# The causal mask of a recurrence's softmax moves from TensorE to VectorE

## The chip, the cores and the metric

One core of one Trainium2 chip runs the kernel. The time is that of the whole kernel on the device, in microseconds (us), as the median of several runs. The engines are called PE (TensorE; PEld is its weight load), DVE (VectorE), ACT (ScalarE), POOL (GpSimd) and SP (SyncE, which here only issues DMAs).

## What is computed

Two attentions over the same x (2048 tokens, 576 features), mixed by a gate. Part A is a recurrence over 64 segments of 32 tokens: each segment attends, together with 8 memory rows, over 40 positions, and the first 8 rows of its output are the next segment's memory. Part B is plain attention with 32 heads of width 18 over all 2048 tokens.

```python
L = M + seg_len                                   # 8 + 32
mask = (idx[:, None] < M) | (idx[:, None] >= idx[None, :])
for s in range(n_seg):                            # 64, one after the other
    h = concat([mem, xs])                         # 40 x 576
    q, k, v = h @ Wq, h @ Wk, h @ Wv              # 32 heads of 128
    scores = where(mask, q @ k.T * scale, -1e9)
    o = (softmax(scores) @ v) @ Wo
    mem = o[:M]
g = sigmoid((x * gate_w).sum(-1, keepdims=True))
return g * A(x) + (1 - g) * B(x)
```

## The kernel before

Everything is recorded first as operations of a planner (`Plan.add`: a name, the engine or engines that may do it, a duration, what it depends on) and then issued. The order on each engine is not found at run time: `ORDER` holds, for PE, DVE, ACT, POOL and SP, a list of numbers that is the sequence of operations (where an operation may go to two engines, the list that it stands in decides). `Plan.run` walks these lists with its constants and durations (`LATE`, `LAG`, `RATES` and those given to `add`), and from this it decides two things only: which operations on PE take the full form of the array and which four columns of 32, and where PE gets a **filler**. `Plan.zeros` adds a filler, one group of matmuls with zero weights on the open sum of part B (L1036 in four columns, L1042 in the full form), wherever by its reckoning PE would stand for at least the filler's length and a margin.

The first 150 us load x and the weights, project part B's q, k and v and write them to memory in DRAM. Then the recurrence runs, some 17.7 us for each of its 64 segments, to about 1285 us, and part B's visits are laid into it: 512 visits of four heads, each of them four score matmuls (L1065, into `sb` and `sp`), two exponentials on ACT (L1074, L1078), four matmuls on the values (L1088, into `ob`). Also in PE's list are the pieces of `last_unit` (L1156, L1160), projections of the last 8 tokens of each segment, which need no memory and are done ahead. At the end the outputs are mixed and stored.

A segment of the recurrence, with the names that the rows show:

- `pvv` (L1437): Q, K and V in pieces, four column groups of 128x32; the tails of the features go in a form of their own (64 rows).
- Q and K are transposed on DVE from `pvv` to `tf` (L1478) and cast into `qk` on POOL or DVE (L1524); V goes through `tm` (L660 on DVE, L658 on ACT) to `v_sb` (L1501, POOL or DVE).
- `psh`: scores, in two halves of 16 heads. One PE step holds the mask's product (L1538, four matmuls of `ident` with `veil`, 320 columns each) and 32 small products (L1546) added to it.
- `et` (L1556): the exponential on ACT, 128x320 in bf16. `pss` (L1567 or L1572): its column sums on PE; `rq` (L1584): reciprocal on DVE; `prb` (L1592): PE spreads it; `et` times `prb` on DVE (L1603).
- `pso` (L1614): weights times V on PE; `ot`: a cast on DVE or ACT; `acc` (L1319): times Wo; `sum` and `obf` (L1346, L1647) add the parts on DVE; `pw` (L1662, L1669): PE turns the new memory, DVE puts it in `ht` (L1678), and the next segment starts.

`veil` is made once: zeros, and -30000 where the mask is false, so that the exponential of a masked score is 0:

```python
nc.tensor.matmul(
    ph[32 * i:32 * i + 32, :], lhsT=ident[:, o:o + 32],
    rhs=veil[:, :].unsqueeze(1).to_broadcast([P, 8, L]),
    start=True, stop=False, ...)
```

DMAs of the loop (`by_head` at L985 for kch, qch and otd; vch, qkd, vld, xg, a_dram) may stand in SP's list or in POOL's.

Of the kernel before, what the change touches and what calls it, by code (L numbers as in the profile page):

```python
# [9 lines left out]
BF16 = mybir.dt.bfloat16  # L10
# [483 lines left out]
def kernel(  # L494
# [15 lines left out]
    nc = tc.nc  # L510
# [1313 lines left out]
    for n in range(NT):  # L1824
        qc, i = divmod(n, 4)
        halves = []
        for hf in range(2):
# [18 lines left out]
            def combine(e, n=n, hf=hf):  # L1846
# [4 lines left out]
                )  # L1851

            halves.append(add(
                f"cb{n}.{hf}", "DVE", psum_copy(288), combine, [a, gates[n]], give=(("pb", a, 0),)
            ))

        def store_out(e, n=n):
# [43 lines left out]
```

## Time and profile before

| what | value |
|---|---|
| runs | 1320.95 us median of 3 (1316.97 to 1321.24) |
| the profiled execution | span 1319.9 us, from its first to its last instruction; no other time of it is given, and the median is 1.05 us above it |
| PE busy | 1287.9 us, 98% |
| ACT busy | 1118.8 us, 85% |
| DVE busy | 796.1 us, 60% |
| POOL busy | 623.2 us, 47% |
[...]

Busy time is the union of an engine's instructions, with the ends of matmuls modelled. What a matmul group takes of PE's queue is therefore read from starts: the distance from its start to that of the next. The idle time of an engine is put down to the instruction that ended it. An engine that idles and is waited for by nobody costs nothing.

### The profile page before, as it was taken

The page shows a single profiled execution, that of the slowest core. Times are in us where ns is not written, and L with a number is a line of the kernel's source. Part 1 is how long each engine was busy: PE and PEld are TensorE (multiplying, and loading weights), DVE is VectorE, ACT ScalarE, POOL GpSimd, SP SyncE. Part 2 cuts the span into 40 slices and gives each one's busy share as a digit, 9 for nine tenths or more (in the row PEclk, how much of TensorE's full clock was granted, in tenths as well). Part 3 has the DMA queues.
Part 4 walks back from the last instruction along what each step waited for, and adds up shares of the span by engine and source line. Part 5 has one row for each costly group of instructions (what it writes and reads, how often), then busy time and mean ns, then how long its engine had stood idle before and what let it go on. Part 6 is the DMA issues. An engine that isn't in the chain of part 4 may idle for free.

```text
span 1319.9 us, 72882 instructions
## 1 busy us (share of the span) xinstructions
PE 1287.9 (98%) x32807; PEld 694.6 (53%) x32807; DVE 796.1 (60%) x1778; ACT 1118.8 (85%) x1343; POOL 623.2 (47%) x1291
## 2 busy tenths in 40 slices
PE   8999999999999999999999999999999999999998
PEld 5444544555555555555555545555555445554445
DVE  3133566666566666655566666666666666666676
ACT  4678989988889888888888888888878989998895
POOL 5461454634653356545553556544436445434430
PEclk9989999999999999999999999999999999999999
DMA  7987512111211022011220112211122111111125
GB/s 233 295 260 245 180 41 57 28 36 33 56 37 42 17 54 57 21 29 35 51 51 26 35 37 45 52 28 34 27 50 64 23 26 25 32 40 23 23 53 182
DMA packets 145064, 88.60 MB, mean 67 GB/s; under 512 B 102439, under 2 KB 135383, under 8 KB 144751
## 3 DMA queue, kind: packets, MB, share of 16 engines
q1 hardware_dynamic: 127527, 51.33, 15.2%
q0 software_dynamic: 15088, 30.41, 7.7%
q8 instruction: 257, 4.21, 1.4%
q10 hardware_dynamic: 2136, 2.19, 0.6%
q14 instruction: 56, 0.46, 0.1%
HBM read 52.74 MB, written 31.12 MB: 64 GB/s over the span
## 4 chain that ended last, share of the span: by engine, by line
PE 86%; DVE 5%; ACT 3%; DMA 3%; issue 2%; POOL 1%; SPq 0%; DVEq 0%; ACTq 0%; POOLq 0%
PE pvv L1437 30%; PE acc L1319 12%; PE sb L1065 11%; PE ob L1088 8%; PE pv L1156 5%; PE pso L1614 3%; PE pq L870 3%; PE pv L1160 3%; ACT etb L1074 2%; PE psh L1546 2%; PE po L1833 1%; PE prb L1592 1%; PE psh L1538 1%; DMA vch<-vgd 1%; DVE v_sb L1501 1%
## 5 line engine op out<-in xcount | busy, mean ns | idle before, releaser
L1074 ACT ACTIVATE etb<-sb 128x1536 bf16<-128x1536 f32 x512 | 743.9, 1453 | 119.6 <-PE sp L1065 89.6
L1078 ACT ACTIVATE etb<-sp 128x512 bf16<-128x512 f32 x512 | 306.4, 598 | 0.8 <-PE sp L1065 0.7
L1501 POOL COPY v_sb<-tm 32x512 bf16<-32x512 bf16 x360 | 224.4, 623 | 140.3 <-DVE tm L660 90.5
L1437 PEld LDWEIGHTS <-ht 128*32 128x32 bf16 (+1 forms) x7680 | 171.6, 94 | 214.4 <-issue 115.0
L1478 DVE STREAM_TRANSPOSE tf<-pvv 128x512 f32<-128x512 f32 x256 | 180.9, 713 | 167.1 <-PE pvv L1437 160.7
L1524 POOL CAST qk<-tf 128x512 bf16<-128x512 f32 x142 | 88.2, 622 | 303.3 <-DVE tf L1478 301.0
L1065 PE MATMUL sb<-qch,kch 32*128 32x512 bf16 x1536 | 201.9, 385 | 4.7 <-ACT etb L1074 2.3
L1065 PE MATMUL sp<-qch,kch 32*128 32x512 bf16 x512 | 196.6, 384 | 2.1 <-DVE vt L660 1.8
L1088 PE MATMUL ob<-etb,vch 128*32 128x512 bf16 x2048 | 193.8, 383 | 1.0 <-DMA vch<-vgd 0.8
L1437 PE MATMUL pvv<-wq_m,ht 128*32 128x512 bf16 x2048 | 163.0, 381 | 0.7
L1437 PE MATMUL pvv<-wk_m,ht 128*32 128x512 bf16 x2048 | 163.0, 381 | 0.2
L1319 PE MATMUL acc<-wo,ot 128*32 128x288 bf16 (+1 forms) x6144 | 160.6, 248 | 1.5 <-DVE ot L660 0.9
L1437 PE MATMUL pvv<-wv_m,ht 128*32 128x512 bf16 x2048 | 155.3, 381 | 0.2
L1319 PEld LDWEIGHTS <-ot 128*32 128x32 bf16 x6144 | 113.8, 97 | 31.9 <-issue 11.7
L1065 PEld LDWEIGHTS <-kch 32*128 32x128 bf16 x2048 | 56.1, 91 | 121.3 <-issue 108.1
L660 DVE CAST ot<-pso 128x320 bf16<-128x320 f32 x192 | 87.6, 485 | 45.9 <-PE pso L1614 44.6
L660 DVE CAST tm<-pvv 128x512 bf16<-128x512 f32 x101 | 69.0, 685 | 46.3 <-PE pvv L1437 43.6
L1088 PEld LDWEIGHTS <-vch 128*32 128x32 bf16 x2048 | 51.6, 95 | 46.2 <-issue 28.5
L1405 POOL COPY qk<-xl 128x128 bf16<-128x128 bf16 x256 | 65.8, 295 | 19.3 <-PE sp L1065 7.5
L1603 DVE TENSOR_TENSOR et<-et,prb 128x320 bf16<-128x320 bf16 x128 | 61.8, 485 | 20.6 <-PE prb L1592 17.4
L1501 DVE COPY v_sb<-tm 32x512 bf16<-32x512 bf16 x152 | 65.6, 432 | 11.7 <-ACT tm L658 9.0
L1556 ACT ACTIVATE et<-psh 128x320 bf16<-128x320 f32 x128 | 55.7, 440 | 17.8 <-PE psh L1546 16.3
(160 smaller groups left out, 1820.6 us busy)
## 6 DMA issues: line engine op xcount, KB each, us to landing
xl<-qkd SPq DMA_DIRECT2D x32, 256.0 KB
qkd<-vl SPq DMA_DIRECT2D x41, 128.0 KB
wo<-in_A_Wo_dram POOLq DMA_DIRECT2D x8, 576.0 KB, 5.8
wq_m<-in_A_Wq_dram POOLq DMA_DIRECT2D x8, 512.0 KB, 6.3
vgd<-vt SPq DMA_DIRECT2D x32, 128.0 KB
wk_m<-in_A_Wk_dram POOLq DMA_DIRECT2D x8, 512.0 KB, 6.9
wv_m<-in_A_Wv_dram POOLq DMA_DIRECT2D x8, 512.0 KB, 6.0
v_sb<-vld SPq DMA_DIRECT2D x128, 32.0 KB
```

What stands on the lines that cost most here:

```text
L660: nc.vector.tensor_copy(out=out_of(), in_=in_of())
L1065: nc.tensor.matmul(sb[:, j, :] if j < 3 else sp[:, :], lhsT=kc[r, o:o + P], rhs=qt_[r, :], start=True, stop=True, tile_position=(32 * j, 0),)
L1074: nc.scalar.activation(out=etb[:, 0:3, :], in_=box["sb", gq, kb][:, :, :], func=ACT.Exp, scale=scale_b)
L1078: nc.scalar.activation(out=etb[:, 3, :], in_=box["sp", gq, kb][:, :], func=ACT.Exp, scale=scale_b)
L1088: nc.tensor.matmul(ob[32 * j:32 * j + 32, :], lhsT=vc[:, o + 32 * j:o + 32 * j + 32], rhs=etb[:, j, :], start=(kb == 0), stop=(kb == NKB - ...
L1156: nc.tensor.matmul(out_, lhsT=lw, rhs=rw, start=(c == 0), stop=(c == NF), skip_group_check=wide)
L1319: nc.tensor.matmul(acc[32 * q:32 * q + 32, :], lhsT=o[:, slot, t0:t0 + CT], rhs=wo[:, h, d:d + n], start=(first and s_ == (s_ % 2 if wide ...
L1405: nc.gpsimd.tensor_copy(out=opened["qk"][:, f, a, 0:16 * L].rearrange("p (u h t) -> p u h t", h=4, t=L)[:, :, :, CT:L], in_=xl[:, f, a, :, ...
L1437: nc.tensor.matmul(o, lhsT=ht[:, c, :], rhs=rw, start=start, stop=stop, tile_position=(r, 32 * j), skip_group_check=True,)
L1478: nc.vector.transpose(out=tf[:, :], in_=box["pvv", s, n][:, :])
L1501: move(out=opened["v_sb"][64 * (j // 2):64 * (j // 2) + CT, o:o + 512], in_=tm[32 * j:32 * j + CT, :],)
L1524: move(out=opened["qk"][:, hf, a, 0:16 * L].rearrange("p (k t) -> p k t", t=L)[:, :, 0:CT], in_=box["tf", s, "QK"[a] + str(hf)][:, :].rear ...
```

## The change

The mask's product leaves the score step: `psh` is 32 matmuls, each of which starts and stops its sum. A constant `cap` takes the place of `veil`: 3.0e38 where the mask is true and 0 where it is false. After the exponential, a new step `kp` on DVE takes the minimum of `et` and `cap`, and the column sums wait for it instead of the exponential. The numbers of `ORDER` and `FULL` are all new, as are some of the planner's constants and durations.

```diff
 ORDER = {
     "PE":
-        "19 15 -5 -5 164 -128 152 -99 -39 210 -159 -75 34 116 -92 -10 45 -3 6 12 -6 -107 10 82 -68 86 -39 33 -21 -49 "
...
     "SP":
...
+        "17 10 14 -2 -2 52 -46 22 22 4 -28 38 -48 24 -10 48 27 12 -27 245 -227 45 -51 234 -225 18 -3 -12 135 -117 3 "
...
-    LAG = {"SP": 0.66, "ACT": 0.66, "POOL": 1.25}
+    LAGS = ({"SP": 0.8, "ACT": 0.8, "POOL": 2.5}, {"SP": 0.66, "ACT": 0.66, "POOL": 1.25})
...
-    RATES = ((300.0, 0.8), (220.0, 0.55))
+    RATES = ((320.0, 1.4), (220.0, 0.55))
...
-    nc.vector.memset(veil[:], 0.0)
+    nc.vector.memset(cap[:], 3.0e38)
...
-        out=veil[0:64, M:L], in_=veil[0:64, M:L], pattern=[[1, seg]],
-        compare_op=ALU.is_gt, fill=-30000.0, base=M + 1, channel_multiplier=-1,
+        out=cap[0:64, M:L], in_=cap[0:64, M:L], pattern=[[1, seg]],
+        compare_op=ALU.is_gt, fill=0.0, base=M + 1, channel_multiplier=-1,
...
+    nc.vector.tensor_copy(out=cap[64:P, :], in_=cap[0:64, :])
...
-                add(f"qd{hf}.{s}", ("DVE", "POOL"), (0.8, 1.33), put_v(hf, (1, 3)), before),
+                add(f"qd{hf}.{s}", ("DVE", "POOL"), (0.9, 1.33), put_v(hf, (1, 3)), before),
...
-                for i in range(4):
-                    o = 32 * (i % 2)
-                    nc.tensor.matmul(
-                        ph[32 * i:32 * i + 32, :], lhsT=ident[:, o:o + 32],
-                        rhs=veil[:, :].unsqueeze(1).to_broadcast([P, 8, L]),
-                        start=True, stop=False, tile_position=(0, 32 * i), skip_group_check=True,
-                    )
...
-                            start=False, stop=True, tile_position=(0, 32 * i), skip_group_check=True,
+                            start=True, stop=True, tile_position=(0, 32 * i), skip_group_check=True,
...
-            p_ = add(f"ph{hf}.{s}", "PE", 0.36, psh, [*turned, pl], mode="col", take=("pb",), pairs=36, drain=0.268)
+            p_ = add(f"ph{hf}.{s}", "PE", 0.227, psh, [*turned, pl], mode="col", take=("pb",), pairs=32, drain=0.268)
...
+            def mask(e, hf=hf):
+                et = opened["et", hf][:, :].rearrange("p (r t) -> p r t", t=L)
+                nc.vector.tensor_tensor(
+                    out=et, in0=et, in1=cap[:, :].unsqueeze(1).to_broadcast([P, 8, L]), op=ALU.min,
+                )
+
+            m_ = add(f"kp{hf}.{s}", "DVE", 0.25, mask, [x_])
...
-            s_ = add(f"sm{hf}.{s}", "PE", 0.08, sm, [x_],
+            s_ = add(f"sm{hf}.{s}", "PE", 0.08, sm, [m_],
...
-            add(f"of{qc}", "SP", 1.9, load_of, [zo, *last["Q"], *deps], dmas=2, kb=590)
+            add(f"of{qc}", "SP", 1.07, load_of, [zo, *last["Q"], *deps], dmas=2, kb=590)
...
-            gates[n] = add(f"ga{n}", ("ACT", "DVE"), (act_time(576), 0.65), mul_a, [la, *last["used"]])
+            gates[n] = add(f"ga{n}", ("ACT", "DVE"), (0.77, 0.51), mul_a, [la, *last["used"]])
```

What this does to the instructions, at three places of the loop. Lines of the changed kernel are a few higher (L1546 becomes L1544, L1592 L1598, L1614 L1620, L1036 L1041, L1603 L1609).

First, DVE in the 51st segment, from the transposes of Q and K to the end of the first half's softmax (`et_1829` and `et_1811` are the first half's tile). Before:

```order
L1478 STREAM_TRANSPOSE tf<-pvv 128x512 x2
L1524 CAST qk<-tf 128x16x32
L1584 RECIPROCAL rq<-pss 107x6
L660 CAST tm<-pvv 128x512
L1603 TENSOR_TENSOR et_1829<-et_1829,prb 128x320
L1501 COPY v_sb<-tm 32x512 x2
```

Now:

```order
L1483 STREAM_TRANSPOSE tf<-pvv 128x512 x2
L1560 TENSOR_TENSOR et_1811<-et_1811,cap 128x320
L1529 CAST qk<-tf 128x16x32
L1590 RECIPROCAL rq<-pss 107x6
L1506 COPY v_sb<-tm 32x512 x2
L1609 TENSOR_TENSOR et_1811<-et_1811,prb 128x320
```

The minimum is new; it waits for ACT's exponential, and the cast to qk that was ahead of this half's reciprocal now stands behind the minimum.

Second, PE at the same place, from the first half's scores to its `pso`; of each group of matmuls the first stands here. Before:

```order
L1546 MATMUL psh<-qk 32x40
...
L1065 MATMUL sb<-qch_120,kch_113 128x512
...
L1437 MATMUL pvv<-wv_m,ht_1817 32x512
...
L1572 MATMUL pss<-bsel,et_1829 32x2
...
L1538 MATMUL psh<-veil,ident 32x320
...
L1592 MATMUL prb<-ident,rq 32x107
...
L1088 MATMUL ob<-etb,vch_116 32x512
...
L1036 MATMUL ob<-ident,nil 32x512
...
L1614 MATMUL pso<-et_1829,v_sb 128x40
```

Now:

```order
L1544 MATMUL psh<-qk 32x40
...
L1442 MATMUL pvv<-wk_m,ht_1799 32x512
...
L1093 MATMUL ob<-etb,vch_113 32x512
...
L1070 MATMUL sb<-qch_117,kch_110 128x512
...
L1041 MATMUL ob<-ident,nil 32x512
...
L1578 MATMUL pss<-bsel,et_1811 32x2
...
L1598 MATMUL prb<-ident,rq 32x107
...
L1620 MATMUL pso<-et_1811,v_sb 128x40
```

The mask's product is gone. Between the scores and the column sums there were one score group and one value piece of V; there are three pieces of K, a values group, a score group and two fillers. A third filler stands between `prb` and `pso`, where there was one.

Third, POOL in the 23rd segment, between two copies of x into `ht`. Before:

```order
L1386 COPY ht_1817<-xg 128x5x24
L1501 COPY v_sb<-tm 32x512 x2
L1524 CAST qk<-tf 128x16x32
L1501 COPY v_sb<-tm 32x512 x6
L1386 COPY ht_1819<-xg 128x5x24
```

Now:

```order
L1391 COPY ht_1799<-xg 128x5x24
L1218 DMA vld<-vl 128x512 x2
L1506 COPY v_sb<-tm 32x512 x2
L1019 DMA vch_115<-vgd 128x4x128
L1720 DMA a_dram<-lbf 4x8x144 x4
L1220 DMA qkd<-vl 128x512
L1506 COPY v_sb<-tm 32x512 x2
```

Eight DMA issues stand there that SP's list held before.

## Rows read from the trace of the kernel before

**Rows 1.** The core's span and its mean granted TensorE clock.

```profile
core 0: 1319.9 us, clock 0.996
```

**Rows 2.** The page: busy us, share of the span, instructions of each engine.

```profile
PE 1287.9 (98%) x32807; PEld 694.6 (53%) x32807; DVE 796.1 (60%) x1778; ACT 1118.8 (85%) x1343; POOL 623.2 (47%) x1291
```

**Rows 3.** Windows: stretch, its length, busy us of each engine, clock, DMA share, GB/s.

```profile
0.00:40.00 40.00, 34.28 (x235) 21.26 (x236) 13.65 (x65) 15.39 (x30) 20.44 (x56) 1.00 0.83 249
40.00:125.00 85.00, 80.62 (x709) 37.93 (x709) 24.53 (x64) 67.67 (x81) 31.89 (x68) 0.96 0.83 269
125.00:150.00 25.00, 24.91 (x397) 14.78 (x398) 11.81 (x27) 22.41 (x24) 6.82 (x12) 1.00 0.63 200
150.00:1285.00 1135.00, 1118.53 (x31082) 600.42 (x31074) 721.78 (x1570) 992.40 (x1187) 562.34 (x1153) 1.00 0.17 39
1285.00:1320.00 35.00, 29.55 (x404) 20.16 (x392) 24.31 (x53) 20.97 (x25) 1.68 (x4) 0.99 0.57 176
```

**Rows 4.** The page: the chain that ended last, by engine.

```profile
PE 86%; DVE 5%; ACT 3%; DMA 3%; issue 2%; POOL 1%; SPq 0%; DVEq 0%; ACTq 0%; POOLq 0%
```

**Rows 5.** Timeline of one segment: start us, us, engine, line, operation, tiles.

```profile
701.00 1.29 DVE L660 CAST tm<-pvv 128x512 bf16<-128x512 f32 x2 [2.10 <-PE pvv L1437]
701.19 0.40 PE L1088 MATMUL ob<-etb,vch 128*32 128x512 bf16 x4
701.41 0.31 PE L1538 MATMUL psh<-veil,ident 128*32 128x320 bf16 x4
701.55 0.41 PE L1546 MATMUL psh<-qk 128*32 128x40 bf16 x32
...
702.40 0.31 PE L1567 MATMUL pss<-bsel,et 128*107 128x2 bf16 x3
702.45 1.28 POOL L1501 COPY v_sb<-tm 32x512 bf16<-32x512 bf16 x2 [2.16 <-DVE tm L660]
702.74 0.20 DVE L1584 RECIPROCAL rq<-pss 107x6 bf16<-107x6 f32 x1 [0.45 <-PE pss L1567]
702.97 1.55 DVE L1501 COPY v_sb<-tm 32x512 bf16<-32x512 bf16 x4
...
705.59 0.39 PE L1036 MATMUL ob<-ident,nil 128*32 128x512 bf16 x4
706.00 0.37 PE L1614 MATMUL pso<-et,v_sb 64*128 64x40 bf16 x16
...
706.63 0.40 PE L1088 MATMUL ob<-etb,vch 128*32 128x512 bf16 x4
706.96 0.37 PE L1614 MATMUL pso<-et,v_sb 64*128 64x40 bf16 x16
...
711.03 0.41 PE L1437 MATMUL pvv<-wk_m,ht 128*32 128x512 bf16 x4
711.25 0.41 PE L1437 MATMUL pvv<-wq_m,ht 128*32 128x512 bf16 x4
711.46 0.41 PE L1437 MATMUL pvv<-wk_m,ht 128*32 128x512 bf16 x4
711.68 0.41 PE L1437 MATMUL pvv<-wq_m,ht 128*32 128x512 bf16 x4
```

**Rows 6.** Groups by line: the mask's product (busy us, mean ns, idle before).

```profile
L1538 PE MATMUL psh<-veil,ident 128*32 128x320 bf16 x512 | 40.1, 301 | 0.0
```

**Rows 7.** Instructions of single lines: duration ns min/median/max, first and last start.

```profile
L1603 DVE TENSOR_TENSOR et<-et,prb x128: 428/486/490, 157.6 to 1286.0; 128x320 bf16<-128x320 bf16 x128
L1124 DVE TENSOR_TENSOR tn<-tq,rtb x32: 649/682/1118, 122.1 to 1306.0; 128x512 bf16<-128x512 f32 x32
L1501 DVE COPY v_sb<-tm x152: 238/368/703, 149.2 to 1281.5; 32x512 bf16<-32x512 bf16 x152
```

**Rows 8.** Groups by line: casts that DVE and ACT share.

```profile
L660 DVE CAST tm<-pvv 128x512 bf16<-128x512 f32 x101 | 69.0, 685 | 46.3 <-PE pvv L1437 43.6 <-POOL qk L1405 2.0
L658 ACT CAST tm<-pvv 128x512 bf16<-128x512 f32 x27 | 15.8, 587 | 7.5 <-PE pvv L1437 4.9 <-issue 2.3
```

**Rows 9.** POOL: DMA issues by line, and its longest wait (us, times, longest).

```profile
L985 POOL DMA_DIRECT2D qch<-qtd x64: 505/505/665, 133.6 to 1227.6; - x64
L1014 POOL DMA_DIRECT2D vch<-vgd x10: 765/779/818, 347.2 to 1162.2; - x10
L1714 POOL DMA_DIRECT2D a_dram<-lbf x12: 587/592/665, 604.7 to 1117.1; - x12
POOL qk L1524 <- DVE tf L1478: 301.0, 105, 11.0
```

**Rows 10.** Groups by line: PE's weight loads for pso, and what they waited for.

```profile
L1614 PEld LDWEIGHTS <-v_sb 64*128 64x128 bf16 x2048 | 39.3, 93 | 39.5 <-issue 24.0 <-POOL v_sb L1501 4.1 <-DVE et L1603 3.0
```

More of the change, by code (lines that the diff above doesn't have):

```diff
@@ L392, in transfer @@
         step = (op.end - op.start) / op.dmas
-        lag = self.LAG[op.eng] if op.lag is None else op.lag
-        rate, after = self.RATES[0 if op.end < self.EARLY else 1]
+        phase = 0 if op.end < self.EARLY else 1
+        lag = self.LAGS[phase][op.eng] if op.lag is None else op.lag
+        rate, after = self.RATES[phase]
         for j in range(op.dmas):
@@ L562 @@
     make_identity(nc, ident[:])
-    veil = const.tile([P, L], BF16, name="veil")
+    cap = const.tile([P, L], BF16, name="cap")
     bsel = const.tile([P, 2], BF16, name="bsel")
@@ L580 @@
     nc.gpsimd.affine_select(
-        out=veil[0:64, M:L], in_=veil[0:64, M:L], pattern=[[1, seg]],
-        compare_op=ALU.is_gt, fill=-30000.0, base=M + 1, channel_multiplier=-1,
+        out=cap[0:64, M:L], in_=cap[0:64, M:L], pattern=[[1, seg]],
+        compare_op=ALU.is_gt, fill=0.0, base=M + 1, channel_multiplier=-1,
     )
     nc.gpsimd.affine_select(
-        out=veil[0:64, 0:M], in_=veil[0:64, 0:M], pattern=[[0, M]],
-        compare_op=ALU.is_gt, fill=-30000.0, base=L, channel_multiplier=-1,
+        out=cap[0:64, 0:M], in_=cap[0:64, 0:M], pattern=[[0, M]],
+        compare_op=ALU.is_gt, fill=0.0, base=L, channel_multiplier=-1,
     )
+    nc.vector.tensor_copy(out=cap[64:P, :], in_=cap[0:64, :])
     selm = ident[:, :].rearrange("p (a b t) -> p b a t", a=2, t=32)[:, :, :, 0:M]
@@ L1510 @@
             pvs.append((
-                add(f"qd{hf}.{s}", ("DVE", "POOL"), (0.8, 1.33), put_v(hf, (1, 3)), before),
-                add(f"qc{hf}.{s}", ("DVE", "POOL"), (0.8, 1.33), put_v(hf, (0, 2)), before),
+                add(f"qd{hf}.{s}", ("DVE", "POOL"), (0.9, 1.33), put_v(hf, (1, 3)), before),
+                add(f"qc{hf}.{s}", ("DVE", "POOL"), (0.9, 1.33), put_v(hf, (0, 2)), before),
             ))
@@ L1529 @@
                 turned.append(add(
-                    f"ct{a}{hf}.{s}", ("POOL", "DVE"), (0.66, 0.45), ct, [ev_a, prev.get(f"psh{hf}")], give=(("tf", ev_a, 0),),
+                    f"ct{a}{hf}.{s}", ("POOL", "DVE"), (0.61, 0.45), ct, [ev_a, prev.get(f"psh{hf}")], give=(("tf", ev_a, 0),),
                 ))
@@ L1853 @@
             halves.append(add(
-                f"cb{n}.{hf}", "DVE", psum_copy(288), combine, [a, gates[n]], give=(("pb", a, 0),)
+                f"cb{n}.{hf}", "DVE", 0.518, combine, [a, gates[n]], give=(("pb", a, 0),)
             ))
```

583 rows, old and new, of tables (FULL, ORDER) are left out of this document.

## The prediction

> **What bounds the kernel now.** One core, so the core's own row is first: 1319.9 us, TensorE's clock granted at 0.996 [rows 1]; the clock is no term here. The busy table comes next: PE 98%, ACT 85%, DVE 60%, POOL 47% [rows 2]. Then the same by stage [rows 3]: PE stands 10.2 us in the first 150 us (5.7, 4.4 and 0.1), 16.5 us in the recurrence (1135.0 less 1118.5), 5.5 us at the end. Last, the chain of waits: 86% of the span is PE, 5% DVE, 3% ACT [rows 4]. So TensorE's queue is what ends last nearly everywhere, and a matmul taken out counts, unless PE then stands where it stood, waiting for the recurrence. The recurrence is one chain through all engines; the rest of PE's queue (scores and values of the other attention, pieces of projections) is laid between its links to cover them. The question is whether cover or chain is short after the change.
>
> All working is against the span, 1319.9; the median of the three runs, 1320.95, is 1.05 higher, and I add the sum to the median.
>
> **Removed: the mask's product.** 512 matmuls from L1538, 128 groups of four beside each other [rows 6]. Their 0.30 us each is a modelled length; what a group takes of the queue is the distance to the next start: 701.41 to 701.55, 0.14 us [rows 5]. 128 x 0.14 = 17.9 us off PE's queue. None of it waited for another engine, so it is all on the path.
>
> **Added on PE: fillers.** The second pair of orders shows the place: where PE had one L1036 group of four before the matmuls on ob and pso, it now has three such groups in the same stretch. Counted over both whole orders, the column form goes from 220 matmuls to 604, so 55 to 151 groups, the full form from 4 to 8: 100 more. A group of four 512-column matmuls takes 0.217 us of the queue (711.03, 711.25, 711.46, 711.68) [rows 5]: +21.6 us. That is more than was removed, and it is the main number against this change: the planner expects PE to stand more often.
>
> **Moved on PE: turns of the array's shape.** A group of values followed by its like costs 0.22 (701.19 to 701.41), followed by the tall shape of pso 0.33 (706.63 to 706.96): a turn is 0.11 us [rows 5]. Counted over the orders, 1565 turns become 1523: 42 x 0.11 = -4.6 us.
>
> **Waits that the fillers take the place of.** A filler is put where PE would have stood. Of the 16.5 us that PE stands in the recurrence [rows 3] I let the 100 new ones cover 13, since they stand ahead of the very links (column sums, pso, fold) at which the page has PE wait; bounds 0 and 16.5. Behind a filler some wait is left: 705.59 to 706.00 is 0.41 where an unhindered step to pso takes 0.33, so 0.08 [rows 5], and 100 of these are +8; bounds 0, and 21.6 if as much again is left behind each as it fills.
>
> **Added on DVE: the minimum.** 128 TENSOR_TENSORs of 128x320 in bf16, both inputs in SBUF. No such row exists. From below, the shortest 512-element SBUF copy, 0.238 us; from above, the same operation on the same tile with one input in PSUM, 0.486 [rows 7]. Nearer is the one DVE operation that reads two SBUF tensors, L1124: 512 elements, 0.649 at least, 0.682 in the middle, 1.118 at most [rows 7]; it shows what meeting a POOL copy does. I take 0.35 us: halfway between the ends, to 0.36, and a little down, since bf16 from SBUF alone runs quicker in these rows. With a handover of about 0.06 (the column sum ends at 702.71, its reciprocal starts at 702.74; the casts of tm end at 702.29 and their copy on POOL starts at 702.45 [rows 5]) a half's path from scores to column sums grows by 0.41. 128 x 0.35 = 45 us more on DVE are no term by themselves: DVE goes from 60% to 64%. [...]
>
> What is queued behind the mask: in the first pair of orders it stands on DVE behind two transposes of tf and ahead of a cast to qk and the reciprocal, so a late exponential holds these. PE's cover was changed to suit: in the shown place PE has a score, a value piece between scores and sums before, and now three pieces of K, a value group, a score group and two fillers. Priced so over 61 middle steps, PE's work between last score and first sum grows by 0.48 us in the first half and 0.27 in the second. The first exceeds 0.41; the second is 0.14 short, and I let a third of 64 second halves feel it: +3 us; bounds 0 and 64 x (0.486 + 0.06 - 0.27) = +18.
>
> **Moved between engines.** 90 operations leave ACT: 21 casts of ot, 13 of tm, 20 of xn, 12 of vt, 9 sums among them; at 0.587, the row of the widest cast [rows 8], that is 53 us at most, ACT to 81%. DVE gets most of them, at 0.685 at most [rows 8] under 62 us: with the masks it ends near 68%. Neither bounds, so nothing; if the cover goes, DVE's queue is late, which is the second rival. 250 DMA issues move from SP's queue, where an issue isn't busy time of an engine that computes, to POOL, at 0.505 (the by-head loads), 0.59 (stores of a_dram), 0.78 (vch) [rows 9]: 40 of kch, 44 of otd, 48 of qch, 64 of a_dram, 24 of qkd, 16 of vch and 14 small ones, some 140 us, POOL from 47% to 58%. POOL has the room: it stands 301 us before its casts of tf alone [rows 9], and PE now waits 4.1 us in all for its copies of v_sb [rows 10]. I cost them at nothing; the cover is that idle time, and the third rival is its loss. The set-up has a longer memset and one copy of 64x40 more, ahead of PE's first work: nothing.
>
> **The ends.** The first 150 us and the last 35 are ordered anew too; PE stands 15.6 us there [rows 3], with DMA engines 0.83 busy in the first 125 us, so most is transfer and stays. I take -1; bounds -8 and +5.
>
> **Sum:** -17.9 - 4.6 + 21.6 - 13 + 8 + 3 - 1 = -3.9 us, 1316 by the span and **1317 us** by the median. The terms nearly cancel: what is removed on PE comes back as fillers. About 0.3% (4 us) is the least that a measurement of this kernel tells from no change.
>
> **Rivals.**
> *The fillers cost less than their length, and the gain stays* (faster). A filler costs nothing where PE would stand anyway. For it: 85% of ACT and 98% of PE leave the chain little that is not already covered, and turns fall too. If half of the 21.6 lies in idle time that the queue had in any case, with no more left behind: -17.9 - 4.6 + 10.8 = -11.7, 1309; with none of it paid, -22.5, 1298. Against: before, fillers were few while PE stood only 16.5 us, so there is little old idle time to lie in.
>
> *The minimum is late* (slower). It reads two SBUF tensors while POOL works half of the time. The rows show the place: four copies of v_sb on DVE beside POOL take 1.55 us, 0.39 each, against 0.238 alone [rows 5, 7], and L1124 is stretched by up to 0.47. With 0.486 for each mask, second halves are short by 0.28, 64 x 0.28 = 18, in place of the +3: +11, 1332; with the same stretch on those that meet POOL in first halves as well, up to 1340. It decides from a mean of about 0.42 us upward. [...]
>
> *POOL's queue* (slower). A copy of v_sb behind four stores of 0.59 comes 2.4 us late, as in the third pair of orders. If one in twelve of the 250 issues puts PE off by a whole 0.55: +11, 1328; one in seven, +20, 1337. Against: the 301 us.
>
> *That the change does not do what it says*: the order has no L1538 matmul left and 128 minima, so only its second half, the fillers, is in question.
>
> **How the numbers follow.** Forecast 0.40, its own range 1310 to 1325: faster by over 4 us in 0.19, within 0.17, slower in 0.04. First rival 0.25: faster 0.23, within 0.02. Late minimum 0.22: within 0.03, slower 0.19. POOL's queue 0.13: within 0.02, slower 0.11. So faster 0.42, same 0.24, slower 0.34. The range goes down to 1301, nearly all of the first rival, and up to 1337, most of the second and third; 0.1 is left outside on either side at most.
>
> **What would show it.** L1036's successor with 604 matmuls at 0.217 apart and PE's idle time in the recurrence below 16 us: the forecast. PE's idle time unchanged or higher, with waits of PE's loads for et's minimum: the second rival, and its duration settles the price (0.35 forecast). PE's loads waiting for v_sb or qk from POOL for tens of us: the third. PE's share well below 98% with a shorter span would show the first. The forecast is wrong if PE's share falls by over a point while the time does not, since the chain, not the queue, would then set the step.

## The result, and the profile after

The changed kernel takes 1338.09 us (median of 4 runs, 1335.32 to 1340.29) against 1320.56 of the kernel before in the same comparison: a ratio of 1.0128, 95% interval 1.0103 to 1.0153. That is 16.9 us more by the ratio (0.0128 x 1320.6), where 3.9 less was forecast, and 1 us above the range. Below, every run is put as its ratio to the kernel before, timed beside it, and as the us that this ratio makes of 1320.6.

The page of the changed kernel begins with its span and its busy table:

```profile
span 1338.6 us, 72840 instructions
PE 1295.8 (97%) x32782; PEld 680.7 (51%) x32782; DVE 888.5 (66%) x2006; ACT 1081.7 (81%) x1253; POOL 764.2 (57%) x1532
```

Against [rows 2] the three helpers moved as the prediction had it (DVE 60% to 66%, ACT 85% to 81%, POOL 47% to 57%). PE is 7.9 us busier, with 17.9 us of work taken out: the fillers add some 21.6 us by the prediction's count. The windows, cut so that the last one is as long as that in [rows 3] (columns as there):

```profile
0.00:40.00 40.00, 31.06 (x205) 18.63 (x205) 25.71 (x88) 4.41 (x6) 15.94 (x36) 1.00 0.76 239
40.00:125.00 85.00, 83.79 (x768) 41.08 (x767) 33.91 (x76) 61.09 (x68) 38.96 (x93) 0.98 0.85 279
125.00:150.00 25.00, 24.89 (x404) 14.65 (x405) 13.99 (x36) 23.38 (x25) 10.98 (x18) 1.00 0.64 188
150.00:1303.00 1153.00, 1124.90 (x30975) 585.46 (x30963) 786.60 (x1744) 975.35 (x1138) 692.24 (x1376) 1.00 0.16 38
1303.00:1339.00 36.00, 31.16 (x448) 20.92 (x444) 28.29 (x65) 17.48 (x20) 6.08 (x10) 0.99 0.56 175
```

In the first 150 us PE stands 10.3 us, as before (10.2), though ACT is less busy there and DVE more. The recurrence has become 18 us longer, and PE stands 28.1 us in it (1153.0 less 1124.9) instead of 16.5, in spite of 100 more fillers. So nearly the whole loss lies there: 11.6 us of it are PE standing, and 6.4 us PE being busier, with those fillers.

The minimum is L1560. The view of that line gives its duration (ns, min/median/max) and who waited for it (us, times):

```profile
L1560 DVE TENSOR_TENSOR et<-et,cap x128: 275/326/775, 154.1 to 1302.1; 128x320 bf16<-128x320 bf16 x128
...
PEld L1578: 17.1, 44
PEld L1573: 5.3, 15
```

Its mean is 429 ns in the view of groups (busy us, mean ns, idle of DVE before it):

```profile
L1560 DVE TENSOR_TENSOR et<-et,cap 128x320 bf16<-128x320 bf16 x128 | 54.7, 429 | 24.3 <-ACT et L1554 22.3
```

PE's loads wait 22.4 us for it at the column sums (the matmuls behind them wait for the same, so theirs are not added). Before, the sums waited for the exponential, by the view of waits:

```profile
PEld L1572 <- ACT et L1556: 7.4, 33, 0.3
PEld L1567 <- ACT et L1556: 2.2, 8, 0.4
```

9.6 us, so 12.8 more. Another link is late as well: the loads of the scores wait 11.9 us for the casts of qk, where the view of waits had 0.6 before:

```profile
PEld L1544 <- POOL qk L1529: 6.9, 14, 2.7
PEld L1544 <- DVE qk L1529: 5.0, 14, 0.6
```

Why the mean is so far above the median shows in the timeline (start us, us, engine, line, what it does):

```profile
604.22 0.44 ACT L1554 ACTIVATE et<-psh 128x320 bf16<-128x320 f32 x1 [0.41 <-PE psh L1544]
604.36 0.83 DVE L1529 CAST qk<-tf 128x512 bf16<-128x512 f32 x1
...
604.97 0.68 POOL L1529 CAST qk<-tf 128x512 bf16<-128x512 f32 x1
605.06 1.45 ACT L1079 ACTIVATE etb<-sb 128x1536 bf16<-128x1536 f32 x1
605.11 0.72 DVE L1560 TENSOR_TENSOR et<-et,cap 128x320 bf16<-128x320 bf16 x1
...
605.88 0.14 PEld L1578 LDWEIGHTS <-et 128*32 128x32 bf16 x12 [0.71 <-DVE et L1560]
...
607.77 1.08 POOL L990 DMA_DIRECT2D qch<-qtd  x2
607.80 0.33 DVE L1560 TENSOR_TENSOR et<-et,cap 128x320 bf16<-128x320 bf16 x1 [0.27 <-ACT et L1554]
```

The first minimum starts while POOL casts qk. POOL ends at 605.65, the minimum at 605.83, 0.18 later; PE's loads stood 0.71 us for it. The second starts beside POOL's DMA issue and takes its 0.33. Over all 128 it is the same: 55 of them take over 0.34 us, each of these starts beside a copy or cast on POOL, and ends 0.171 to 0.184 us after it.

The same rows show a second delay. The first exponential ends at 604.66, and its minimum starts at 605.11, since DVE is still at a cast to qk. Over the 128 (ends and starts in the trace) the minimum starts 0.03 us after its exponential in the middle but 0.25 in the mean; 52 start more than 0.15 late, behind DVE's copies, transposes and casts.

### The profile page after: what moved, and what is told of

Read it like the earlier page. It is cut to its first block, busy times and chain, and to the rows that moved or that the text cites. A ratio compares the mean times of both kernels' runs of the same rounds, so it can differ in the third digit from the quotient of the medians.

```text
span 1338.6 us, 72840 instructions
## 1 busy us (share of the span) xinstructions
PE 1295.8 (97%) x32782; PEld 680.7 (51%) x32782; DVE 888.5 (66%) x2006; ACT 1081.7 (81%) x1253; POOL 764.2 (57%) x1532
## 4 chain that ended last, share of the span: by engine, by line
PE 45%; DVE 5%; ACT 1%; issue 1%; POOL 1%; DMA 0%; SPq 0%; DVEq 0%; ACTq 0%; POOLq 0%
PE pvv L1442 18%; PE acc L1324 7%; PE sb L1070 6%; PE ob L1093 4%; PE pso L1620 2%; PE po L1839 1%; PE pv L1161 1%; PE psh L1544 1%; DVE v_sb L1506 1%; PE pv L1165 1%; PE prb L1598 1%; PE ob L1041 1%; ACT etb L1079 1%; DVE et L1560 1%; DVE et L1609 1%
## 5 line engine op out<-in xcount | busy, mean ns | idle before, releaser
L1093 PE MATMUL ob<-etb,vch 128*32 128x512 bf16 x2048 | 190.6, 383 | 1.4 <-issue 0.9
L1529 POOL CAST qk<-tf 128x512 bf16<-128x512 f32 x131 | 83.2, 639 | 168.0 <-DVE tf L1483 163.3
L1324 PE MATMUL acc<-wo,ot 128*32 128x144 bf16 (+1 forms) x6144 | 161.6, 247 | 2.5 <-issue 2.2
L1442 PE MATMUL pvv<-wv_m,ht 128*32 128x512 bf16 x2048 | 158.2, 381 | 0.2
L665 DVE CAST ot<-pso 128x320 bf16<-128x320 f32 x213 | 96.5, 483 | 37.8 <-PE pso L1620 36.2
L665 DVE CAST tm<-pvv 128x512 bf16<-128x512 f32 x114 | 78.0, 685 | 39.2 <-PE pvv L1442 36.3
L1560 DVE TENSOR_TENSOR et<-et,cap 128x320 bf16<-128x320 bf16 x128 | 54.7, 429 | 24.3 <-ACT et L1554 22.3
L665 DVE CAST vl<-pv 128x512 bf16<-128x512 f32 x71 | 48.5, 686 | 31.5 <-PE pv L1161 18.5
```

The costliest lines, as they stand in the source:

```text
L665: nc.vector.tensor_copy(out=out_of(), in_=in_of())
L1093: nc.tensor.matmul(ob[32 * j:32 * j + 32, :], lhsT=vc[:, o + 32 * j:o + 32 * j + 32], rhs=etb[:, j, :], start=(kb == 0), stop=(kb == NKB - ...
L1324: nc.tensor.matmul(acc[32 * q:32 * q + 32, :], lhsT=o[:, slot, t0:t0 + CT], rhs=wo[:, h, d:d + n], start=(first and s_ == (s_ % 2 if wide ...
L1442: nc.tensor.matmul(o, lhsT=ht[:, c, :], rhs=rw, start=start, stop=stop, tile_position=(r, 32 * j), skip_group_check=True,)
L1529: move(out=opened["qk"][:, hf, a, 0:16 * L].rearrange("p (k t) -> p k t", t=L)[:, :, 0:CT], in_=box["tf", s, "QK"[a] + str(hf)][:, :].rear ...
L1560: nc.vector.tensor_tensor(out=et, in0=et, in1=cap[:, :].unsqueeze(1).to_broadcast([P, 8, L]), op=ALU.min,)
```

## The experiments

Three theories: **L**, the minimum lengthens the recurrence's chain, and the chain, not PE's queue, sets the step; **O**, the new orders and fillers cost the time whatever masks; **P**, POOL's 250 more DMA issues make it late.

**Without any mask, in the new orders**

```diff
-                nc.vector.tensor_tensor(
-                    out=et, in0=et, in1=cap[:, :].unsqueeze(1).to_broadcast([P, 8, L]), op=ALU.min,
-                )
```

> Leaves the mask out of the computation: the changed kernel with its orders and fillers, without the minimum on DVE and without the mask's product on PE. Theory L (the minimum lengthens the recurrence: it takes 0.43 us in the mean, stretched by POOL's work, and what is queued behind it on DVE comes late): the time falls by 12 to 20 us, to 1318 to 1326, PE's waits for the column sums go from 12 back to about 3 us and those for the scores from 9.7 to under 5. Theory O (the new orders and fillers cost the time, whatever the mask is): falls by under 5 us. Theory P (POOL's queue with 250 more DMA issues makes the casts of qk late): falls by under 7 us, with PE's waits for the scores still near 9.

Measured: 1323.55 us median, ratio 1.0004 (0.9983 to 1.0025), +0.5. Taking the minimum away gives back 16.4 us, as theory L had it. But the kernel is then no faster than the one before, with 17.9 us less on PE's queue and nothing in its place. The loads' waits for qk mostly stay (4.8 and 3.9 us for POOL's and DVE's casts), so these belong to the orders more than to the minimum, and theory L's under 5 for them was missed:

```profile
PEld L1544 <- POOL qk L1529: 4.8, 11, 1.8
PEld L1544 <- DVE qk L1529: 3.9, 14, 0.5
```

How far the new orders hold the sums back without any minimum can be read from the trace, from the end of each exponential to the first matmul of its sums: in the mean 0.95 us in first halves and 0.72 in second ones, against 0.49 and 0.50 in the kernel before. With the minimum it is 1.02 and 0.84, so the minimum itself adds 0.07 and 0.11, some 12 us over 64 segments, of the 16.4. Where the rest arises (on DVE, behind the minimum, for one) no run takes apart.

**The old mask in the new orders**

```diff
...
+                for i in range(4):
+                    o = 32 * (i % 2)
+                    nc.tensor.matmul(
+                        ph[32 * i:32 * i + 32, :], lhsT=ident[:, o:o + 32],
+                        rhs=veil[:, :].unsqueeze(1).to_broadcast([P, 8, L]),
+                        start=True, stop=False, tile_position=(0, 32 * i), skip_group_check=True,
+                    )
...
-                nc.vector.tensor_tensor(
-                    out=et, in0=et, in1=cap[:, :].unsqueeze(1).to_broadcast([P, 8, L]), op=ALU.min,
-                )
```

> The changed kernel's orders and fillers with the old mask: the product on PE is back, the minimum is gone. Against the run without either it tells what 17.9 us of PE's queue are worth in these orders. Theory L: if the recurrence and not PE's queue sets the step, under 9 us more than without either, so 1322 to 1333, still below the changed kernel. If PE's queue sets the step, 15 to 18 us more, 1334 to 1343. Theory O: 1345 or more, the changed kernel and the product's 18 us less the little that the minimum cost.

Measured: 1332.73 us, ratio 1.0075 (1.0049 to 1.0101), +9.9. Two things follow. The product's 17.9 us of queue make 9.4 us of time here (1.0075 less 1.0004, each with some 3 us either way), about half: at the edge of theory L's 9, and far from the 15 to 18 of a queue that sets the step. And the new orders with the old mask are 9.9 us worse than the old orders with it. They leave room for a longer link from scores to sums (the sums stand as late as without a mask, 0.99 and 0.71 us behind their exponential); that this room is the cost is argued, not shown. Theory O is right by that much, though its own number, over 1345, was not met.

**Without fillers**

```diff
     def zeros(self, op, est, mode):
+        return None
```

> The changed kernel without any filler: 604 matmuls in columns and 8 in the full form are gone, all else is as it was. Theory O (fillers are paid): falls by 20 to 33 us. Theory L (they lie in time in which PE waits for the recurrence): within 5 us of the changed kernel, and PE's waits for column sums, pso and fold grow by about 30 us. If the granted clock falls below 0.99, longer by more than 5.

Measured: 1336.55 us, ratio 1.0108 (1.0078 to 1.0138), not to be told from the changed kernel's 1.0128. PE's busy time falls by 27 us, its standing time grows by as much (most of it ahead of pso, the scores of part B and the fold (`pw`), and only 1 us ahead of the sums), and the total does not change:

```profile
PE 1268.6 (95%) x32170; PEld 674.5 (50%) x32170; DVE 887.9 (66%) x2006; ACT 1081.5 (81%) x1253; POOL 762.9 (57%) x1532
```

So fillers lie in time in which PE waits anyway. The granted clock is 0.995 without them and 0.997 with them, so in this kernel they neither cost nor bring anything that can be told from noise.

**DMA issues back on SP**

```diff
 def queue(e):
-    return nc.gpsimd.dma_start if e == "POOL" else nc.sync.dma_start
+    return nc.gpsimd.dma_start if e == "POOL" and plan.now.name not in BACK else nc.sync.dma_start
```

(`BACK` holds the names of the 110 operations.)

> The changed kernel, with the DMA issues of 110 operations (272 issues) that stood in SP's list before issued by SP again, at the place in the program where POOL's list has them. Theory P: falls by 8 to 15 us, PE's waits for the scores from 9.7 to under 3 us. Theory L: within 4 us, waits for the scores over 7 us, since it is DVE's transposes and casts behind the minimum that are late. POOL's busy time falls by 130 to 150 us in either.

Measured: 1338.06 us, ratio 1.0115 (1.0076 to 1.0154). POOL's busy time falls by 155 us to the following, and the time does not move:

```profile
PE 1293.6 (97%) x32782; PEld 680.4 (51%) x32782; DVE 888.3 (66%) x2006; ACT 1081.5 (81%) x1253; POOL 609.2 (46%) x1260
```

Theory P falls. PE's waits for the casts of qk did fall, for POOL's from 6.9 to 2.8 us by its loads, without the time following.

**No mask in the old orders**

```diff
-                for i in range(4):
-                    o = 32 * (i % 2)
-                    nc.tensor.matmul(
-                        ph[32 * i:32 * i + 32, :], lhsT=ident[:, o:o + 32],
-                        rhs=veil[:, :].unsqueeze(1).to_broadcast([P, 8, L]),
-                        start=True, stop=False, tile_position=(0, 32 * i), skip_group_check=True,
-                    )
...
-            p_ = add(f"ph{hf}.{s}", "PE", 0.36, psh, [*turned, pl], mode="col", take=("pb",), pairs=36, drain=0.268)
+            p_ = add(f"ph{hf}.{s}", "PE", 0.227, psh, [*turned, pl], mode="col", take=("pb",), pairs=32, drain=0.268)
```

> Leaves the mask out of the computation: the kernel before with its orders, without the mask's product and without a minimum; fillers are set again by the planner. What the removal alone can give. If PE's queue sets the time: 14 to 18 us less than before, 1303 to 1309. If the recurrence sets it (theory L, as 9 us for the product's return in the new orders suggest): 3 to 10 us less, 1313 to 1320, with PE's waits over 0.04 us grown from 44 us by most of the rest. If PE's queue is no limit at all: within 3 us of before.

Measured: 1316.14 us, ratio 0.9968 (0.9950 to 0.9987), -4.2. This is the run that decides about the sum: of 17.9 us off PE's queue, in the orders that were set with them in place, 4.2 reach the end, as theory L had it (3 to 10). (The planner puts 13 more fillers there, 2.8 us, and PE's standing time grows by 3.4, less than theory L had said.) PE's queue is 97% busy and sets the time only in a small part.

```profile
PE 1278.9 (97%) x32347; PEld 682.4 (52%) x32347; DVE 796.0 (61%) x1778; ACT 1117.2 (85%) x1343; POOL 623.8 (48%) x1291
```

It is also the most that any other way of masking could gain in the old orders.

**The minimum in the old orders**

```diff
...
+            m_ = plan.float(f"kp{hf}.{s}", "DVE", 0.25, mask, [x_])
...
+            head = self.ready(queues["DVE"][-1], "DVE") if queues["DVE"] else None
+            for op in self.floats:
+                at = self.ready(op, "DVE")
+                if at is not None and (head is None or at <= head):
+                    queues["DVE"].append(op)
+                    self.floats.remove(op)
+                    break
...
```

> The kernel before with its orders, the product taken out and the minimum put in: the planner's walk places each minimum on DVE as soon as the exponential is done by its reckoning, and sets fillers again; nothing else is reordered. Theory O (the new orders lose): 1330 or less, better than the changed kernel by 8 us or more. Theory L (the orders had to make room for a longer link, and did so as well as could be): 1336 to 1350, with PE's waits for the column sums over 20 us.

Measured: 1372.36 us, ratio 1.0391 (1.0369 to 1.0412), +51.6: outside both expectations, on theory L's side. The sums' waits (us, times) show where it lies:

```profile
L1570 DVE TENSOR_TENSOR et<-et,cap x128: 278/326/769, 157.6 to 1335.5; 128x320 bf16<-128x320 bf16 x128
...
PEld L1588: 46.8, 67
...
PEld L1583: 18.6, 29
```

In orders without room for it, PE's loads stand 65.4 us for the minimum. Part of this is the place that the walk gives it: it starts 0.38 us after its exponential in the mean, most often behind a copy to v_sb on DVE. The new orders are 35 of the 52 us better than that, and still not good enough.

**Half a minimum, and two**

```diff
-                    out=et, in0=et, in1=cap[:, :].unsqueeze(1).to_broadcast([P, 8, L]), op=ALU.min,
+                    out=et[:, 0:4, :], in0=et[:, 0:4, :], in1=cap[:, :].unsqueeze(1).to_broadcast([P, 4, L]), op=ALU.min,
```

> Leaves half of the mask out of the computation: in the changed kernel the minimum is taken over four of the eight heads of each partition, 160 elements. Theory lock (a minimum that meets a copy on POOL is held until that copy ends and then 0.175 us more): the shortest falls from 0.275 to about 0.2 us, the longest stay near 0.67, the mean falls by only 0.03 to 0.06, and the time by 1 to 4 us. Theory length (the minimum's own elements are what is late): the mean falls by 0.1 or more, the longest too, and the time by 5 to 8 us.

> The changed kernel with each minimum taken twice, which changes no value: one more instruction of 0.33 to 0.45 us on the same link. Theory L (the link from the exponential to the column sums is on the path in a large part of the 128 halves): 10 to 20 us more, 1348 to 1358, as taking the minimum away gave 14.5. If the link is covered by the fillers and other work in most segments: under 5 us more.

Measured: half 1328.50 us, ratio 1.0066 (1.0040 to 1.0091), +8.7; twice 1384.89 us, ratio 1.0482 (1.0457 to 1.0507), +63.6. The groups of the half, and the second of the two:

```profile
L1560 DVE TENSOR_TENSOR et<-et,cap 128x160 bf16<-128x160 bf16 x128 | 42.5, 333 | 25.2 <-ACT et L1554 23.3
```

```profile
L1563 DVE TENSOR_TENSOR et<-et,cap 128x320 bf16<-128x320 bf16 x128 | 62.0, 484 | 4.4
```

The half's durations (ns, min/median/max):

```profile
L1560 DVE TENSOR_TENSOR et<-et,cap x128: 195/243/691, 156.2 to 1292.1; 128x160 bf16<-128x160 bf16 x128
```

The half takes 0.096 us less in the mean, 12.2 us over all 128, and gives 8.2. The second minimum adds 62.0 us and costs 46.7, far over both expectations. So above the half's length each us of minimum costs 0.67 to 0.75 us of time; below it, from 0.333 in the mean to none, 42.6 us give only 8.2. Up to some length PE's cover holds. If nothing is paid up to there and 0.7 beyond, it is 0.24 us in the mean (an estimate from these four runs; none lies between 0.333 and no minimum), about the 0.25 that the planner reckons with. Nor is the minimum on the path everywhere: in the changed kernel the sums start within 0.15 us of its end in 62 of the 128 halves, in the run with two in 101.

For the half, the mean and the time came near to theory length (at least 0.1, and 5 to 8 us), while the shortest, 0.195, and the longest, 0.691, are as theory lock had them. Both act. What theory lock had wrong is its fixed 0.175 us: of the half, a held one ends about 0.09 us after POOL's copy, so what is left to do by then shrinks with the minimum. Counted from its own middle length (over 0.26 us), 48 of 128 are held, against 55.

**Copies on POOL that read little**

```diff
-                    move(
-                        out=opened["v_sb"][64 * (j // 2):64 * (j // 2) + CT, o:o + 512],
-                        in_=tm[32 * j:32 * j + CT, :],
-                    )
+                    if e == "DVE":
+                        move(out=opened["v_sb"][r:r + CT, o:o + 512], in_=tm[32 * j:32 * j + CT, :])
+                        continue
+                    move(out=opened["v_sb"][r:r + CT, o:o + 8], in_=tm[32 * j:32 * j + CT, 0:8])
+                    nc.gpsimd.memset(opened["v_sb"][r:r + CT, o + 8:o + 512], 0.0)
```

> Leaves most of V out of the computation: in the changed kernel each copy to v_sb that POOL does becomes a copy of 8 columns and a memset of the other 504, so that POOL reads SBUF for a short part of the time and writes it as before. Theory lock (a minimum that starts while POOL copies from SBUF to SBUF is held until the copy ends): the minimum's mean falls from 0.43 to under 0.37 us, its longest cases beside v_sb copies vanish, and the time falls by 5 to 10 us beyond what the same edit gives in the kernel before. Theory bandwidth (DVE and POOL writing at once slow each other, or the length is DVE's own): the mean stays within 0.03 of 0.43, the time follows the control.

> Control: leaves most of V out of the computation in the kernel before, by the same edit. It has no minimum. Its DVE copies from SBUF (v_sb, casts of tf) may be held less: a few us. Both theories: 0 to 6 us less than before; if more than 8, POOL's copies themselves were on the path, and the other run must be read against it.

Measured: in the changed kernel 1330.69 us, ratio 1.0085 (1.0055 to 1.0116), +11.2, so 5.7 us less; in the kernel before 1322.92 us, ratio 1.0010 (0.9989 to 1.0031), no change. The views of groups (busy us, mean ns):

```profile
L1561 DVE TENSOR_TENSOR et<-et,cap 128x320 bf16<-128x320 bf16 x128 | 42.2, 331 | 25.3 <-ACT et L1555 23.4
...
L1510 POOL MEMSET v_sb<- 32x504 bf16 x362 | 185.3, 512 | 0.1
L1509 POOL COPY v_sb<-tm 32x8 bf16<-32x8 bf16 x362 | 72.3, 200 | 133.5 <-DVE tm L665 107.0 <-DVE rq L1591 5.9 <-ACT tm L663 4.8
```

POOL is as long at v_sb as it was (0.71 us for 0.63), but the minimum's mean falls from 0.429 to 0.331, and 9 of 128 are over 0.34 us. Of the 34 that start beside a memset none is held. For the minimum's length theory lock is shown, by these 9 against 55 and by the 34: what holds the minimum here goes with what POOL reads, not with what it writes. For the time it is less sure, since the interval of this run overlaps that of the changed kernel (1.0103 to 1.0153).

**A smaller minimum**

```diff
-        nc.vector.memset(bsel[64 * jj:64 * jj + 64, jj:jj + 1], 1.0)
+        nc.vector.memset(bsel[64 * jj:64 * jj + L, jj:jj + 1], 1.0)
...
-                    out=et, in0=et, in1=cap[:, :].unsqueeze(1).to_broadcast([P, 8, L]), op=ALU.min,
+                    out=et[:, :, M:L], in0=et[:, :, M:L], in1=cap[:, M:L].unsqueeze(1).to_broadcast([P, 8, L - M]), op=ALU.min,
```

> The changed kernel with a smaller minimum that computes the same: it leaves out the 8 memory columns of each head, which are masked nowhere but in rows that belong to no key, and the column sums count 40 rows of each 64 instead. 256 elements for 320. By the slope of the runs with a half minimum and two (0.8 us of time for each us that all minima together take): the mean falls by 0.03 to 0.05 and the time by 3 to 5 us, to 1333 to 1335. If only minima that POOL holds cost time: under 2 us.

Measured: 1334.00 us, ratio 1.0097 (1.0063 to 1.0132), +12.8. The group's mean is 387 ns:

```profile
L1560 DVE TENSOR_TENSOR et<-et,cap 128x256 bf16<-128x256 bf16 x128 | 49.4, 387 | 24.8 <-ACT et L1554 23.0
```

That is 5.3 us less over all, and 4.1 us of time, which agrees with the slope; but its interval overlaps that of the changed kernel, so the gain is not shown. It stays behind the kernel before, as does every run here that takes a minimum.

## Why the prediction was wrong

**The step that failed** is the first term: "128 x 0.14 = 17.9 us off PE's queue. None of it waited for another engine, so it is all on the path." It is off the queue, and its size is right (0.141 us in the mean of the 128 groups), but in the old orders 4.2 us of it were on the path (no mask, old orders) and in the new ones 9.4. That PE waited for nobody at the product does not put it on the path: a shorter queue reaches the recurrence's next link sooner and is held there. The two profiled executions in the old orders lie 7.0 us apart; of the rest, 2.8 are new fillers, 3.4 more standing time of PE, and 3.1 longer score steps, whose loads now wait 3.1 us for the casts of qk (0.6 before). With that, the rest of the sum's PE terms fall too. The fillers' +21.6 are nothing: without a single filler the time is the same. The -13 of waits that they should have taken over, and the +8 behind them, went the other way: PE's idle time in the recurrence rose by 11.6 us. The turns' -4.6 were not tested alone. That the terms "nearly cancel" was a balance of a queue that set the time only in part.

**The minimum's term** was mis-sized: +3, from 0.35 us with a third of the second halves short. The minimum measured 0.326 in the middle and 0.429 in the mean, and the runs put its price at 16.4 us (changed kernel less no mask, same orders): 5.7 for POOL's holds (0.098 us each, intervals overlapping) and 10.7 for the rest. With 0.331, the mean beside POOL's short copies, the prediction's own working would give 64 x (0.331 + 0.06 - 0.27) = 7.7 if every second half felt it, so the length is not all of it. Its handover of 0.06 was too short: it is 0.25 from exponential to minimum, because DVE is at other work. No run tested what that costs. That 0.35 was near this 0.331 did not help, since the stretch was known from [rows 7] and left for a rival.

**What was right.** The rival "The minimum is late" happened in its mechanism and its sign: minima that meet POOL's copies are stretched (55 of the 128), and the mean, 0.429, is above its deciding point of 0.42. (Of the rows that the prediction names for the stretch, the copy's 0.39 us against 0.238 has one input; L1124, 0.649 to 1.118, has two, like the minimum, and the four of its 32 that take 1.016 us or more each start beside a copy or cast on POOL.) It had a chance of 0.22. That its price of 1332 to 1340 holds the 1338 is in part luck. Its 18 us for the minimum are near the 16.4 measured, but the stretch, which sets this rival off, makes 5.7 of these by the runs; and the 18 are added to the same sum of queue terms, -6.9 us by the prediction, where the new orders without a mask measure +0.5. PE's work between scores and sums did grow as reckoned (0.48 and 0.27; the sums stand 0.46 and 0.22 later without a minimum). POOL's queue costed at nothing, the ends at about nothing, and the shares of DVE, ACT and POOL were right. The test named for the second rival, PE's idle time higher with loads waiting for et's minimum, is what the profile shows.

**The balance**, from the runs: no mask in the old orders -4.2; the same in the new orders +4.7 (to +0.5; these two intervals just touch, and the orders' cost is clearer with the old mask, +9.9); the minimum unheld +10.7; held by POOL +5.7: together +16.9. The first carries some 3 us either way, the others, differences of two ratios, 4 to 5, so the second and the last are hardly clear of noise; the minimum's 16.4 as a whole is clear of it. Why the new orders cost time with a short link is argued only: more of PE's other work stands between scores and sums, and 90 operations went from ACT, most of them to DVE. No run took that apart; of what was moved, only the DMA issues were put back.

## What to carry to other kernels

A queue that is 98% busy need not be the limit when its idle moments have been filled with other work (here 17.9 us off it gave 4.2 us of time): before costing a removal, ask what the engine would do with the time, and try the removal alone, which here takes one deletion. Work moved from a full engine onto a chain costs most of its length past the cover, some 0.7 us for each us here, while the work that it replaced may have cost far less (0.23 us for each us of the product in the old orders, 0.53 in the new). Price the link as it will run: with the time until the new engine is free for it (0.25 us in the mean here), and, where it meets copies on POOL as this minimum did (POOL 57% busy), with the mean over all 128, 0.429 us, not with its middle, 0.326.

## What was not expected of the hardware

The 55 minima that POOL's copies and casts held were not slowed in proportion: each ended 0.171 to 0.184 us after the copy, whether 0.17 or 0.60 us of it were left (0.72 us in the rows at 605.11, against 0.33 a moment later). That time went with the minimum's length: about 0.175 us for 320 elements, 0.14 for 256 and 0.09 for 160, and the longest took 0.775, 0.740 and 0.691 us. A TENSOR_TENSOR on the same tile with one input in PSUM shows none of this in the changed kernel, though 65 of its 128 start beside a copy or cast on POOL (these take 0.483 us in the mean, as do the other 63):

```profile
L1609 DVE TENSOR_TENSOR et<-et,prb x128: 448/487/490, 156.3 to 1305.3; 128x320 bf16<-128x320 bf16 x128
```

DMA issues on POOL do not hold the minimum: the 19 that started beside one took 0.28 to 0.33 us. And 155 us of POOL's time, in DMA issues, moved to SP without a trace in the total (a ratio of 1.0115 against 1.0128).
